# Attention into a gated channel mix: keys and gates from token pairs and projected values

## The chip, the cores and the metric

The kernel runs on one core of one Trainium2 chip. The core has five engines that work side by side, each through its own queue in order: PE (TensorE, matrix products into PSUM), DVE (VectorE) and ACT (ScalarE), which read PSUM and SBUF and write to either, POOL (GpSimd), which here only issues loads, and SP (SyncE), which issues stores. The metric is device time in microseconds, the median of several runs. PSUM has eight banks, each 512 fp32 numbers wide on 128 partitions; whatever PE makes must be read out of a bank before the bank can be used again.

## What is computed

Shapes: 8 batches, 8 heads, 576 tokens, head size 64, 32 memory slots a head. The first half is an attention over memory slots:

```python
a = exp(phi - max(phi)); a = a / a.sum(over slots)     # per token, slot
k_m = einsum('bhsm,bhsd->bhmd', a, k)                  # 32 keys a head
v_m = einsum('bhsm,bhsd->bhmd', a, v)                  # 32 values a head
attn = softmax(q @ k_m.T / 8)                          # 576 x 32 a head
x = (attn @ v_m), heads side by side                   # 576 x 512 a batch
```

The second half is a channel mix, in which every token is mixed with the token before it (zeros before the first):

```python
xk = mu_k * x + (1 - mu_k) * x_prev
xr = mu_r * x + (1 - mu_r) * x_prev
k = relu(xk @ w_k)               # 512 -> 1024, the "keys"
v = (k * k) @ w_v                # 1024 -> 512, the "values"
out = sigmoid(xr @ w_r) * v      # the "gates", 512 -> 512
```

## The kernel before

The order of all work is written out by hand in PLAN, one word a step; a step that has several parts (products, then a read-out, then a second read-out) stands there once for each part. `3:s` is batch 3's score step, `c2:5s` block 5 (of 8) of the keys of chunk 2, `g:7` the gate and `o:7` the value of output tile 7, `p:k:4` the load of k of batch 4, `0:busy7_2` seven filler products. BANKS gives each product's PSUM bank. Steps run on an engine in this order, so a waiting step holds back all behind it on its engine. Loads go through POOL's queue (lines 137, 141, 172, 184), the first of phi and k through ACT's (137, 150), stores through SP's (589), the last ones in turn through SP's and ACT's.

Attention of a batch. The 8 heads are split in two groups c of four; four heads of 32 slots make 128 rows. `exp_phi` (L256, ACT) makes the unnormalised weights `em`. `ekv` (L280) makes slot keys and values, 72 products of 64 x 32 of the array. `esum` (L290) sums the weights, `norm_k`/`norm_v` (L316, L327) scale by the reciprocal. `tr_k` (L346) turns the keys, `turn_q` (L365, DVE) turns q. `scores` (L378) makes 32 products of 32 x 32 of the array and four exponentials of 288 elements (L386, ACT). From batch 1 on the softmax is normalised on DVE: `fold_e` turns the exponentials (L412), `fold_sum` adds and inverts (L418, L419), `fold_out` turns the result back (L424), `weigh` multiplies (L431), twice. Batch 0 takes another way, which is shorter when the engines are idle: `denom` sums on PE (L394), a logarithm and an exponential on ACT (L402, L407) invert.

Channel mix of batches 1 to 7. `values` (L337) makes x = attn @ v_m: eight products of 32 x 64 of the array, twice (the first 320 and the last 256 tokens), and x is copied to SBUF (L445). `diff` (L457, L458, DVE) forms x - x_prev, `mix` scales it by mu - 1 (L468 on ACT or L470 on DVE) and adds x (L472): this gives xkT and xrT, rings of four batches with the 512 features on partitions. Batch 0 skips this: `norm_mu`/`norm_both` (L482, L496) put mu into the slot values, and `mixed` (L337) makes xk and xr directly, which are copied out (L518).

`key` (L604): for 128 of the 1024 key features and up to 512 tokens, four products of 128 x 128 of the array, one for each 128 of the 512 features; then relu (L610 DVE or L612 ACT) and square (L619 ACT or L621 DVE) into `sq`. Chunks after batch 0 are 512 tokens whatever the batch. `gate` (L637): four products of 512 columns for 128 tokens, then tanh (L641, ACT; the sigmoid as a tanh). `value` (L654): eight products of 512 columns for 128 tokens, then one DVE instruction multiplies by the gate (L660), and `store` writes the rows, usually as two pieces of 64.

Of the kernel before, what the change touches and what calls it, by code (L numbers as in the profile page):

```python
# [18 lines left out]
PLAN = [  # L19
    "0:c00d 0:exp1 0:busy1_5 0:exp0 0:q0 0:c01a 0:busy13_9 0:z 0:busy7_2 0:z 0:kg0 p:q:0h 0:mu 0:busy2_3 0:c10d",  # L20
    "0:c11a 0:kg1 0:busy2_1 0:ak 0:busy1_e0 0:tk 0:busy1x7_e2b 0:q1 0:busy1_4 0:busy1x4_4b 0:tk 0:s0 0:s0 0:s1",
    "0:busy1x6_5b p:v:0g 0:s1 0:vg0 0:busy1x5_3b 0:mu 0:l0 0:l0 0:l1 0:mub 0:mub p:v:0h 0:vg1 0:nm1 0:nm0",
    "0:busy1x4_e1b 0:l1 0:r0z 0:w0 0:l2 0:l2 0:busy1x4_2b 0:h2z 0:y2 0:busy1x4_e0b 0:l3 0:l3 0:busy2_e1 0:h3z",
    "0:busy5_0 0:busy2_e0 0:y3 0:mk0 0:uk0d 0:mk1 0:uk0a 0:uk1d p:wk:0-4 c0:0as p:wk:4-8 c0:0as c0:0as 0:mr0 0:ur0a",
    "0:ur0d c0:1av c0:1av c0:1av c0:3av c0:3av c0:3av c0:2a 0:uk1a p:phi:1 1:exp 0:mr1 0:ur1a c0:4bs 0:ur1d c0:6as",
    "c0:6as c0:6bs c0:6bs c0:6bs 1:z 1:z p:k:1 1:k c0:4bs c0:2b c0:2a 1:ak c0:4bs c0:2a c0:3b p:q:1 c0:3b 1:q0 c0:3b",
    "c0:4as 0:busy1x7_e1b c0:4as c0:4as 1:tk 1:tk c0:1bs c0:1bs c0:7as c0:7as 1:q1 c0:5av 1:s c0:7as c0:5av c0:5av",
    "c0:6as 1:s 1:s c0:0bs c0:7b 1:fe 1:fs 1:fo p:wv:0-2 p:wr:0-4 c0:1bs c0:7b c0:7b p:v:1 1:w0 p:wv:2-4 o:0a o:1a",
    "1:w1 0:tb p:phi:2 c0:5b p:k:2 c0:5b c0:2b c0:2b c0:5b g:1 g:1 g:0 g:0 o:0a g:3 g:3 o:1a c0:0bs 1:v 1:av g:2 1:x0",
    "p:v:2 c0:0bs 1:x0 o:3a 1:x0 1:xv1 1:xv1 o:2b o:0b o:3a o:2a o:1b 1:xv1 2:exp 1:dd 1:k0d 1:k0d 2:z 2:z 1:k2e",  # L30
    "1:k2e o:3b g:2 c1:0s c1:0s c1:0s c1:4 c1:4 p:q:2 c1:6 c1:6 c1:5s c1:5s c1:5s c1:3v 2:kv 2:ak o:0b o:3b 2:av o:2b",
    "1:r2d c1:7s c1:7s 2:tk 1:r0d 1:r0d 1:r2d c1:6 c1:7s c1:3v c1:3v 2:q0 2:q1 c1:2 c1:2 g:7 2:tk 2:s c1:4 2:s 2:s",
    "g:7 c1:1s c1:1s c1:1s p:q:3 p:v:3 p:phi:3 g:6 g:8 p:k:3 g:5 g:5 3:exp o:1b c1:2 o:7 o:2a 3:q1 2:fe 2:fs 2:fo",
    "2:w1 2:w0 o:7 o:5 o:5 3:z g:6 g:8 3:z 2:x1 2:x1 2:x1 g:4 2:xv0 p:phi:4 3:kv 3:q0 2:xv0 p:q:4 o:4 3:av 2:xv0 g:4",
    "3:ak 3:tk 2:dd 2:k2e p:phi:5 4:exp 3:tk o:6 2:k0d 2:k0d 3:s 3:s 3:s 2:k2e c2:5s c2:5s c2:4v c2:5s c2:2s c2:6s",
    "c2:6s c2:6s c2:0s c2:0s c2:0s 2:r2d c2:3s c2:3s 2:r0d 2:r0d p:v:4 3:fe c2:3s 2:r2d g:10 3:fs c2:7 c2:2s c2:7 o:6",
    "3:fo o:4 g:11 g:11 3:w1 3:w0 c2:1v g:10 g:9 c2:1v c2:1v c2:7 c2:4v 4:z 4:z 4:q0 c2:4v p:k:4 3:x0 g:12 g:9 3:x0",
    "3:x0 4:kv 3:x1 c2:2s o:11 4:q1 3:x1 3:x1 3:dd 3:k0d 3:k0d o:8 4:av o:11 o:8 o:10 5:exp 4:ak 4:tk 4:tk 5:z 5:z",
    "3:k2e 3:k2e p:v:5 p:k:5 5:kv 4:s g:12 5:ak 5:av c3:0s c3:6s 4:s 4:s 3:r0d 3:r0d o:10 p:q:5 3:r2e 5:q0 5:tk 5:tk",
    "5:q1 c3:4s c3:4s 4:fe 4:fs c3:0s 3:r2e c3:1 5:s 5:s 5:s 5:fe c3:1 p:phi:7 c3:5 c3:0s c3:1 4:fo c3:4s 4:w1 c3:7s",  # L40
    "c3:3s c3:3s c3:3s c3:5 g:14 4:w0 g:14 c3:7s c3:7s c3:2s o:9 o:9 g:16 c3:2s c3:2s c3:6s c3:6s g:13 g:13 4:x0 c3:5",
    "o:14 5:fs 5:fo 5:w0 5:w1 4:x0 4:x0 o:14 g:16 o:15 p:q:6 p:v:6 6:q1 7:exp 4:x1 4:x1 4:x1 4:dd o:13 o:13 4:k0d 7:z",
    "p:v:7 7:z 4:k0d 5:x0 5:x0 5:x0 g:17 p:phi:6 o:12 o:12 4:k2e 4:k2e 5:xv1 g:17 5:xv1 5:xv1 6:q0 5:dd 5:k0d 5:k2d",
    "5:k0d 5:k2d g:15 g:15 6:exp c4:6s c4:6s c4:6s o:15 c4:2s c4:2s c4:2s c4:3s c4:3s p:k:6 c4:0 c4:0 c4:1 c4:1 6:z",
    "6:z 4:r2d 6:kv c4:3s p:k:7 7:kv 7:ak 6:nk 7:av c5:1s c4:5s c4:1 c5:1s c5:1s c4:0 c5:2s 4:r2d c5:2s 6:nv 6:tk",
    "6:tk 5:r0d c4:5s c4:5s c4:4 c4:4 c4:7s c4:7s c4:7s 7:tk 7:tk 6:s 4:r0d c4:4 o:16 4:r0d g:18 p:q:7 7:q1 7:q0 6:s",
    "6:s 6:fe 6:fs 6:fo c5:0s 7:s 5:r2e 5:r2e 5:r0d c5:0s 7:s c5:2s c5:3 c5:6s 6:w1 6:w0 c5:3 o:16 c5:7s c5:0s c5:7s",
    "c5:7s 7:s 7:fe g:20 c5:4v g:19 g:19 c5:3 o:19 o:19 g:20 c5:6s c5:4v c5:4v c5:6s o:17 o:17 6:x1 6:x1 7:fs 7:fo",
    "7:w0 c5:5s c5:5s c5:5s g:18 7:w1 6:x1 o:18 o:18 o:20 o:21 6:xv0 6:xv0 6:xv0 6:dd 6:k0d 6:k0d 6:k2d 6:k2d g:25",
    "g:25 7:x1 7:x1 o:20 7:x1 o:22 7:xv0 7:xv0 g:21 g:21 o:21 7:xv0 7:dd g:23 g:22 c6:0s g:23 c6:7s 6:r0e 6:r0e 6:r2e",  # L50
    "6:r2e c6:1 7:k0d c6:4s c6:4s c6:2v c6:2v 7:k0d 7:k2e c6:3s c6:0s c6:2v g:22 c6:0s 7:k2e o:23 o:22 c6:1 c6:1 g:26",
    "c7:0s c7:0s c6:5s o:23 g:30 c6:6s g:26 c8:1 c7:0s c6:4s c6:7s c6:7s c6:5s c6:5s c7:3 c8:1 g:27 c6:3s c7:1 c6:6s",
    "g:29 c6:3s g:27 g:24 g:24 c6:6s c7:3 c7:5s c7:3 c7:2 c8:6v c7:2 c7:2 7:r2e 7:r2e o:26 o:26 c7:4 c7:4 o:24 c7:5s",
    "o:25 c7:4 c7:5s c8:6v g:28 c8:1 g:30 7:r0e o:24 c8:5 c8:6v 7:r0e g:32 g:35 o:25 c7:1 c8:5 c8:4s c8:4s c8:2 c8:4s",
    "c7:7 c7:1 c8:5 c7:7 g:29 c7:6 c7:6 g:31 g:31 c7:7 c7:6 o:31 o:31 o:29 o:27 c8:7 o:27 g:35 g:34 g:34 c8:2 c8:2",
    "c8:3 c8:3 c8:3 o:29 c8:0 c8:0 c8:0 g:28 o:28 o:28 g:32 o:30 o:30 c8:7 c8:7 o:34 g:33 o:33 o:32 o:34 g:33 o:33",
    "o:32 o:35 o:35 o:35 o:35",
# [3 lines left out]
BANKS = (  # L61
    "0123456701243051623405471624371236745201367452167541260371462317054637105463710472104572630457260340"
    "1401473501473514762305714602357162034576034573425103472503614736145073142507316407216403176240517624"
    "3017620147632014736201475301462537401625301631251760231572460374260374203201574572361527035417521524"
    "7610541534156450643257"
)

PRE = "q:0g id:"
SUMS = ()


NJ = 9
# [5 lines left out]
def kernel(  # L78
# [25 lines left out]
    HALVES = (slice(0, 5 * QR), slice(5 * QR, S))  # L104
    CT = 512
    STARTS = (0,) + tuple(range(S, NTOK, CT))

# [6 lines left out]
    banks = iter(BANKS)  # L114

    def ps_tile(shape, dtype, name):
        bank = next(banks, None)
        return psum.tile(shape, dtype, name=name, tag="ps" + (bank or ""), bufs=1 if bank else 8)
# [28 lines left out]
    k0 = []  # L147
    for gs in (slice(0, 2), slice(2, 4)):
        k0.append(work.tile([128, 2, NJ, D], F32, name="k0f", tag="x", bufs=3))
        nc.scalar.dma_start(out=k0[-1].rearrange("p h j d -> p h (j d)"), in_=rows(k[0])[:, gs])  # L150
# [60 lines left out]
    RING = 4 * S  # L211
    xk_T = big.tile([128, ND, RING], BF16, name="xkT")
    xr_T = big.tile([128, ND, RING], BF16, name="xrT")
    sq = big.tile([128, NF, 2 * S], BF16, name="sq")

    def keep_busy(n, blocks=CT // 64):

        ps = ps_tile([128, CT], F32, "idle")[:, :blocks * 64]
        for _ in range(n):
            nc.tensor.matmul(ps.rearrange("p (a b) -> p a b", b=64), lhsT=zeros,  # L220
                             rhs=zeros[:, :64].unsqueeze(1).to_broadcast([128, blocks, 64]), start=True, stop=True,
                             skip_group_check=True)
# [13 lines left out]
    def load_mu():  # L236
        ps_mu = ps_tile([128, 2 * ND], F32, "psmu")
        nc.tensor.transpose(ps_mu, mu2, ident_f)
        yield
        nc.vector.tensor_scalar_add(mu1, ps_mu, -1.0)  # L240

    def attention(b):
        st = {}

        def half_tile(hf, name):
            sl = HALVES[hf]
            return ps_tile([128, sl.stop - sl.start], F32, name)

        x0 = b * S % RING
# [8 lines left out]
        def cast_k(gs, eng):  # L258

            def go():  # L260
                dst, src = kv5[:, 0, gs], k0[gs.start // 2][:, gs.start % 2:gs.start % 2 + gs.stop - gs.start]
                if eng == "a":
                    nc.scalar.copy(dst, src)
                else:
                    nc.vector.tensor_copy(dst, src)
            return go
# [19 lines left out]
        def esum():  # L286
            st["zps"] = ps_tile([128, 2], F32, "zps")
            parts = [em[:, j].rearrange("p h m -> p (h m)") for j in range(NJ)] if b not in SUMS else st["es"]
# [6 lines left out]

        def sum_rows():

            left = work.tile([128, HH * M], F32, name="es", tag="es", bufs=1)
            nc.vector.reduce_sum(left, em.rearrange("p j h m -> p (h m) j"), axis=mybir.AxisListType.X)
            terms = work.tile([128, 3, HH * M], BF16, name="et", tag="et", bufs=1)  # L300
            for i in range(3):
# [132 lines left out]
        def values(hf, both=False):  # L434

            def go():
# [3 lines left out]
                for i in range(ND):  # L440
                    if i % 2 == 0:
                        yield
# [276 lines left out]
```

## Time and profile before

Three runs took 201.34, 201.42 and 201.59 us, median 201.42. The profile is of one execution, whose span from the first to the last instruction is 199.2 us; what lies around the span is not in it (2.2 us against the median).

| engine | busy us | share of the span | instructions |
|---|---|---|---|
| PE, products | 192.4 | 97% | 2188 |
| PE, weight loads (beside products) | 101.7 | 51% | 2211 |
| DVE | 145.1 | 73% | 302 |
| ACT | 142.6 | 72% | 320 |
| POOL | 28.8 | 14% | 43 |

| group | engine | count | busy us |
|---|---|---|---|
| keys, L604 | PE | 344 | 67.7 |
| values, L654 | PE | 319 | 65.3 |
| gates, L637 | PE | 138 | 35.2 |
| filler, L220 | PE | 122 | 15.5 |
| relu, L612 | ACT | 71 | 38.0 |
| tanh, L641 | ACT | 36 | 21.2 |
| gate times value, L660 | DVE | 41 | 24.8 |

How to read it: busy time is a union, in which overlapping instructions count once; a few records of products are missing (344 of 352 for the keys). The mean time of one instruction is from its start to its own end, and neighbours overlap, so a rate is read from one start to the next. A tile shape such as 64*32 is the part of the array that a product uses. In the table by stretches the columns are the stretch, its length, the busy time (and count) of PE, PEld, DVE, ACT and POOL, PE's granted clock, the DMA share and GB/s; in the timeline, the start, the time covered, engine, line, operation, tiles and count.

### The profile page before, as it was taken

Reading aid. Unit: us, or ns where it says so; the run is one execution under the profiler, and the core shown is the slowest. Engines: PE = TensorE matmul, PEld = TensorE weight load, DVE = VectorE, ACT = ScalarE, POOL = GpSimd, SP = SyncE. Lnnn points to the kernel's source line nnn. Section 1 sums busy time; section 2 is a strip of 40 time slices with the busy share of each in tenths; the row PEclk is TensorE's granted clock in tenths of the full one; section 3 lists DMA queues with packets and bytes.
Section 4 is the critical chain, followed back from the end, with each engine's and each line's share of the span. In section 5 each row is a group of like instructions: output and inputs, shape, how many; then the busy total and the mean of one; then the engine's idle time right before and its main releaser. Section 6 shows DMA issues by size and latency. Waiting matters only on the chain.

```text
span 199.2 us, 5369 instructions
## 1 busy us (share of the span) xinstructions
PE 192.4 (97%) x2188; PEld 101.7 (51%) x2211; DVE 145.1 (73%) x302; ACT 142.6 (72%) x320; POOL 28.8 (14%) x43
## 2 busy tenths in 40 slices
PE   8999999999999999999999999999999999999992
PEld 8445677675444445544446854443444444444451
DVE  2046858898999999999999989997996037232541
ACT  3337899858868899799979999753778978343310
POOL 7553411410117100270000000000000000000000
PEclk9999999999999999999999999999999999999998
DMA  6999999999999999999997010062042202404454
GB/s 205 274 206 263 211 204 203 265 228 225 248 281 293 266 207 252 263 251 255 250 233 188 17 44 0 16 146 53 0 107 56 54 0 65 95 3 105 105 127 137
DMA packets 24521, 31.88 MB, mean 160 GB/s; under 512 B 1960, under 2 KB 19120, under 8 KB 24496
## 3 DMA queue, kind: packets, MB, share of 16 engines
q0 software_dynamic: 16848, 20.32, 53.6%
q1 hardware_dynamic: 6176, 8.92, 17.5%
q10 hardware_dynamic: 1472, 2.29, 3.3%
q8 instruction: 17, 0.28, 0.5%
q14 instruction: 8, 0.07, 0.1%
HBM read 38.28 MB, written 9.44 MB: 240 GB/s over the span
## 4 chain that ended last, share of the span: by engine, by line
PE 84%; DMA 10%; DVE 1%; ACT 1%; issue 1%; POOL 0%
PE pk L604 28%; PE pv L654 26%; PE pr L637 14%; DMA ph<-in_phi_dram 10%; PE idle L220 7%; PE kvps L280 3%; PE nops L337 1%; PE scps L378 1%; DVE xkT L472 1%; PE mxps L337 1%; PE zps L290 1%; ACT em L256 1%; PE ktps L346 1%; ACT sg L641 0%; DVE mu_d L470 0%
## 5 line engine op out<-in xcount | busy, mean ns | idle before, releaser
L604 PE MATMUL pk<-xkT,wk 128*128 128x512 bf16 (+4 forms) x344 | 67.7, 340 | 0.7 <-DVE xkT L472 0.3
L654 PE MATMUL pv<-wv,sq 128*128 128x512 bf16 (+3 forms) x319 | 65.3, 352 | 0.4
L604 PEld LDWEIGHTS <-wk 128*128 128x128 bf16 x352 | 32.8, 98 | 28.1 <-issue 1.8
L654 PEld LDWEIGHTS <-sq 128*128 128x128 bf16 x328 | 31.3, 98 | 29.8 <-issue 0.2
L612 ACT ACTIVATE rl<-pk 128x512 bf16<-128x512 f32 (+3 forms) x71 | 38.0, 555 | 10.8 <-PE pk L604 10.4
L637 PE MATMUL pr<-wr,xrT 128*128 128x512 bf16 x138 | 35.2, 379 | 0.5 <-ACT sg L641 0.2
L660 DVE SCALAR_TENSOR_TENSOR o<-sg,pv 128x512 f32<-128x512 f32 (+3 forms) x41 | 24.8, 616 | 10.8 <-PE pv L654 10.2
L641 ACT ACTIVATE sg<-pr 128x512 f32<-128x512 f32 x36 | 21.2, 597 | 14.0 <-PE pr L637 9.9
L621 DVE TENSOR_TENSOR sq<-rl 128x512 bf16<-128x512 bf16 (+5 forms) x45 | 14.6, 344 | 18.5 <-ACT rl L612 17.6
L619 ACT ACTIVATE sq<-rl 128x512 bf16<-128x512 bf16 (+5 forms) x59 | 26.8, 488 | 0.9
L637 PEld LDWEIGHTS <-xrT 128*128 128x128 bf16 x144 | 13.6, 98 | 16.1 <-DVE xrT L472 0.2
L445 ACT CAST x<-nops 128x256 bf16<-128x256 f32 (+1 forms) x46 | 15.2, 413 | 7.1 <-PE nops L337 7.1
L468 ACT ACTIVATE mu_d<-diff,mu 128x576 bf16<-128x576 bf16 x22 | 15.8, 782 | 1.7 <-DVE diff L458 1.4
L220 PE MATMUL idle<-zeros 128*128 128x64 bf16 (+4 forms) x122 | 15.5, 293 | 1.0 <-DVE zeros L151 1.0
L365 DVE STREAM_TRANSPOSE qT<-q 128x576 uint32<-128x576 uint32 x16 | 12.1, 764 | 4.2 <-DMA q<-in_q_dram 4.2
L386 ACT ACTIVATE e<-scps 128x288 bf16<-128x288 f32 x32 | 10.6, 413 | 1.9 <-PE scps L378 1.9
L431 DVE TENSOR_TENSOR atn<-e,lz 128x576 bf16<-128x576 bf16 (+2 forms) x17 | 11.4, 716 | 0.1
L470 DVE TENSOR_SCALAR mu_d<-diff,mu 128x576 bf16<-128x576 bf16 x34 | 11.3, 382 | 0.1
L256 ACT ACTIVATE em<-ph 128x1152 bf16<-128x1152 f32 (+1 forms) x9 | 9.5, 1070 | 2.6 <-DMA ph<-in_phi_dram 2.6
L457 DVE TENSOR_TENSOR diff<-x 128x1024 bf16<-128x1024 bf16 (+1 forms) x21 | 10.4, 552 | 0.7 <-ACT x L445 0.2
L472 DVE TENSOR_TENSOR xrT<-x,mu_d 128x1152 bf16<-128x1152 bf16 x14 | 10.2, 745 | 1.0 <-ACT mu_d L468 0.9
L220 PEld LDWEIGHTS <-zeros 128*128 128x128 bf16 x122 | 8.3, 120 | 5.0 <-issue 1.1
(68 smaller groups left out, 149.1 us busy)
## 6 DMA issues: line engine op xcount, KB each, us to landing
out_dram<-o SPq DMA_DIRECT2D x59, 128.0 KB, 2.4
ph<-in_phi_dram POOLq DMA_DIRECT2D x7, 576.0 KB, 18.8
kv<-in_k_dram POOLq DMA_DIRECT2D x7, 576.0 KB, 17.7
q<-in_q_dram POOLq DMA_DIRECT2D x7, 576.0 KB, 19.9
kv<-in_v_dram POOLq DMA_DIRECT2D x7, 576.0 KB, 16.2
k0f<-in_k_dram ACTq DMA_DIRECT2D x2, 576.0 KB, 7.0
wk<-in_moe_w_k_dram POOLq DMA_DIRECT2D x2, 512.0 KB, 13.3
wv<-in_moe_w_v_dram POOLq DMA_DIRECT2D x2, 512.0 KB, 18.8
```

The source lines that it names most:

```text
L220: nc.tensor.matmul(ps.rearrange("p (a b) -> p a b", b=64), lhsT=zeros, rhs=zeros[:, :64].unsqueeze(1).to_broadcast([128, blocks, 64]), sta ...
L445: (nc.vector.tensor_copy if both and i > 1 else nc.scalar.copy)(st["x"][:, i, sl], pss[i])
L468: nc.scalar.activation(t[:, i], st["d"][:, pr + i, :], AF.Copy, scale=mu1[:, o:o + 1])
L472: nc.vector.tensor_add(dst, st["x"][:, pr:pr + n], t)
L604: nc.tensor.matmul(pk[:, p0 - lo:p1 - lo], lhsT=wk_sb[:, di, fi * 128:(fi + 1) * 128], rhs=xk_T[:, di, p0 % RING:p0 % RING + p1 - p0], sta ...
L612: nc.scalar.activation(rl, pk, AF.Relu, scale=HALF ** 0.5)
L619: nc.scalar.activation(sq[:, fi, p:p + p1 - p0], rl[:, part], AF.Square)
L621: nc.vector.tensor_mul(sq[:, fi, p:p + p1 - p0], rl[:, part], rl[:, part])
L637: nc.tensor.matmul(pr, lhsT=xr_T[:, di, c0:c0 + 128], rhs=wr_sb[:, di, :], start=(di == 0), stop=(di == ND - 1))
L641: nc.scalar.activation(gated[t], pr, AF.Tanh, scale=0.5)
L654: nc.tensor.matmul(pv[:, cols], lhsT=sq[:, fi, p:p + 128], rhs=wv_sb[:, fi, cols], start=(fi == 0), stop=(fi == NF - 1))
L660: nc.vector.scalar_tensor_tensor(o[:, cols], in0=gated[t][:, cols], scalar=1.0, in1=pv[:, cols], op0=AL.add, op1=AL.mult)
```

## The change

The keys and gates of batches 1 to 7 are no longer computed from x. With A the softmax weights of a token (256 numbers, 8 heads x 32 slots) and V the slot values, x = A V, so xk @ w_k = A G0 + A_prev G1, where G0 = V (mu w_k), Gs = V w_k and G1 = Gs - G0. Tokens are taken in pairs (a, b), where p is the token before a: b's result is A_a Gs + (A_b - A_a) G0, and a's is A_a Gs + (A_p - A_a) G1. The product A_a Gs is shared, so a pair takes three products over 256 slots instead of two over 512 features.

- `tr_v` turns the slot values, `project` multiplies them with w_k, w_r (Gs) and with mu w_k, mu w_r (G0), six steps a batch, each eight products of 64 x 32 of the array and 512 columns into two banks; `keep_g` copies each bank into `G` on ACT or DVE; `other_g` subtracts G1 on DVE (three a batch). `scale_w` makes mu w_k and mu w_r once, on DVE.
- The tokens of batches 1 to 7 stand in two halves of 288, all a's and all b's: `exp_scores` writes the exponentials in that order, 16 instructions of 64 or 80 elements a batch in place of 4 of 288. `steps_between` forms the two differences of weights (DVE, four instructions).
- `pair_key`: two products of 288 columns make the shared part in one bank; ACT or DVE copies it to a second bank; two products more go onto each bank. `relu` then reads each bank by itself, `square` takes both at once. `pair_gate` is the same for 128 pairs and 512 columns. The last 32 tokens of each half do not fill a tile: `rest_gate`, and `value` for tiles named e0 to e3, take those of two batches together, four pieces of 32 columns of the array each.
- Removed for these batches: `values` into x, `diff`, `mix`, the rings xkT and xrT. Kept for batch 0: `mixed`, keys and gates from x0T.
- Batch 0's scores, exponentials, logarithms and products go by token halves and not by head groups (`s0`, `s1`, `es00` ...). Filler products after the warm-up run: 16 in place of 44.
- An output tile of batches 1 to 7 is stored as four pieces of 32 rows. The last steps (TAIL) use SP's and ACT's queue in turn.
- All steps have a new place, bank and engine in PLAN (`c2:1/a@4`: on ACT, bank 4); the loads have a new order, and wk comes in three pieces.

The diff, cut to its core:

```diff
-    "1:w1 0:tb p:phi:2 c0:5b p:k:2 c0:5b c0:2b c0:2b c0:5b g:1 g:1 g:0 g:0 o:0a g:3 g:3 o:1a c0:0bs 1:v 1:av g:2 1:x0",
...
+    "2:s@5602 2:G00@41 2:es1 g:11 2:E000/d 2:es0 t:111 g:10@0 2:Gs0@24 s:16/d 2:G02@56 t:110 2:fe p:k:4 o:11@7 2:fs",
+    "2:fo g:10/a@3 g:10 2:Es01/a o:13@4 2:w0 2:E021/a o:12@6 2:E020/a o:13 t:101 2:w1 o:11 t:100 2:Es00/a c2:1@0",
+    "c2:2@2 2:Gs2@34 2:E001/a 2:D0 2:Gs1@15 o:e0@7 4:exp 2:Es21/d 2:Es11/a 2:Es10/a c2:1/a@4 2:Es20/a 2:G01@15 o:12",
...
+            if b:
+                e = st["e"][:, c].rearrange("p (r v u) -> p r v u", r=2, u=PB)
+                for w in range(2):
+                    ps = st["sc", 0][c, w].rearrange("p j (u r) -> p r j u", r=2)
+                    for r, vs, js_ in EVEN_ODD:
+                        nc.scalar.activation(e[:, r, vs, w * PB // 2:(w + 1) * PB // 2], ps[:, js_[0], js_[1]],
+                                             AF.Exp, scale=scale)
...
+        def project(v, i):
+            def go():
+                pss = [ps_tile([128, CT], F32, "gps", cover=CT) for _ in range(2)]
+                w = ((wk_sb, wr_sb), (mwk, mwr))[v == 0][i == 2]
+                cols = GCOLS[i % 2] if i < 2 else slice(0, Dm)
+                for g in range(HH):
+                    m = slice(g * M, (g + 1) * M)
+                    for c in range(2):
+                        nc.tensor.matmul(pss[c][m], lhsT=st["vT"][ROWS[c], m], rhs=w[ROWS[c], g, cols],
+                                         start=True, stop=True, skip_group_check=True)
...
+        def keep_g(v, i, c):
+            return lambda: copier()(g_tile()[:, v, c, GCOLS[i]], st["gps", v, i][c])
+        def other_g(i):
+            return lambda: nc.vector.tensor_sub(g_tile()[:, 1, :, GCOLS[i]], g_tile()[:, 2, :, GCOLS[i]],
+                                                g_tile()[:, 0, :, GCOLS[i]])
+        def steps_between():
+            d = st["d"] = work.tile([128, 2, 2, NP], BF16, name="diff", tag="diff", bufs=2)
+            a = st["at"].rearrange("p c (r i) -> p c r i", r=2)
+            nc.vector.tensor_sub(d[:, 1], a[:, :, 1], a[:, :, 0])
+            nc.vector.tensor_sub(d[:, 0, :, PB:], a[:, :, 1, :NP - PB], a[:, :, 0, PB:])
...
-                        nc.tensor.matmul(pk[:, p0 - lo:p1 - lo], lhsT=wk_sb[:, di, fi * 128:(fi + 1) * 128],
-                                         rhs=xk_T[:, di, p0 % RING:p0 % RING + p1 - p0],
-                                         start=(di == 0), stop=(di == ND - 1))
...
+    def pair_key(b, fi):
+        def go():
+            f = slice(fi * 128, (fi + 1) * 128)
+            pa = ps_tile([128, NP], F32, "pk", cover=NP)
+            for c in range(2):
+                nc.tensor.matmul(pa, lhsT=st["G"][:, 2, c, f], rhs=st["at"][:, c, :NP], start=c == 0, stop=False,
+                                 skip_group_check=True)
+            yield
+            pb = ps_tile([128, NP], F32, "pb", onto=NP)
+            copier()(pb, pa)
+            yield
+            for ps, (v, kind) in zip((pa, pb), SHIFTS):
+                for c in range(2):
+                    nc.tensor.matmul(ps, lhsT=st["G"][:, v, c, f], rhs=st["d"][:, kind, c], start=False, stop=c == 1,
+                                     skip_group_check=True)
...
+    def rest_gate(n):
...
+            for k in range(4):
+                for w in range(4):
+                    nc.tensor.matmul(ps[w * PB:(w + 1) * PB], lhsT=terms[w][k][0], rhs=terms[w][k][1], start=k == 0,
+                                     stop=k == 3, skip_group_check=True)
...
+            b, (h, r) = int(name[0]), divmod(int(name[1]), 2)
+            for v in range(4):
+                parts.append((out[b].rearrange("(u x) d -> x u d", u=PB)[8 * h + 2 * v + r], v * PB, PB))
+        for n, (dst, p, rows_) in enumerate(parts):
+            queues[n % len(queues)].dma_start(out=dst[:, cols], in_=o[p:p + rows_, cols])
```

## The prediction

> **What bounds the kernel now.** I read the page's busy shares and slices first, then the busy time by stretches, then the timeline. The page:
> ```profile
> span 199.2 us, 5369 instructions
> ...
> PE 192.4 (97%) x2188; PEld 101.7 (51%) x2211; DVE 145.1 (73%) x302; ACT 142.6 (72%) x320; POOL 28.8 (14%) x43
> ...
> PE   8999999999999999999999999999999999999992
> ```
> PE is full in every slice, so two things count: the work that PE must do, and what makes it wait. The stretches (busy time of PE, PEld, DVE, ACT, POOL) show PE full even where the others nearly are:
> ```profile
> 20.00:60.00 40.00, 39.28 (x587) 24.37 (x587) 33.96 (x71) 32.99 (x78) 8.58 (x12) 1.00 1.23 234
> 60.00:100.00 40.00, 39.58 (x520) 18.88 (x525) 38.96 (x74) 36.48 (x88) 9.45 (x13) 1.00 1.17 254
> ```
> From 60 to 100 us DVE is busy 38.96 of 40 us and ACT 36.48, and PE still 39.58. The timeline gives prices; I take them from one start to the next, since neighbours overlap:
> ```profile
> 94.77 1.89 PE L637 MATMUL pr<-wr,xrT 128*128 128x512 bf16 x8
> 96.58 0.34 PE L337 MATMUL nops<-atn,vb 32*64 32x320 bf16 x8
> 96.86 3.63 PE L654 MATMUL pv<-wv,sq 128*128 128x512 bf16 x15
> ...
> 47.80 0.80 PE L280 MATMUL kvps<-kv,em 64*32 64x128 bf16 x72
> ...
> 84.84 0.52 ACT L327 ACTIVATE vb<-kvps,rz 128x64 bf16<-128x64 f32 x2
> 85.24 1.33 ACT L386 ACTIVATE e<-scps 128x288 bf16<-128x288 f32 x4
> 86.40 1.49 ACT L468 ACTIVATE mu_d<-diff,mu 128x576 bf16<-128x576 bf16 x2
> ...
> 95.91 1.35 DVE L418 TENSOR_REDUCE se<-eT 128x36 f32<-128x1152 bf16 x1
> 97.29 0.38 DVE L419 RECIPROCAL se<-se 128x36 f32<-128x36 f32 x1
> 97.70 1.38 DVE L424 STREAM_TRANSPOSE lz<-se 128x1152 f32<-128x1152 f32 x1
> ```
> A 512-column product costs 0.216 us (8 `pr` with 0.09 behind them in 1.81), so 0.422 ns a column. Eight tiled `nops` of 320 columns take 0.28, not 8 x 0.135: they run side by side. 72 `kvps` of 128 columns take 0.73, where nine rounds of eight side by side are 0.49: eight 64x32 tiles run together too. A tiled run costs a fixed 0.23 (0.09 ahead of it, 0.14 after). ACT: four `e` of 288 elements from PSUM in 1.16, so 0.29; 512 take 0.48; hence 0.05 + 0.84 ns an element. DVE: 512 from PSUM 0.60, the 1024 bf16 `diff` 0.60, a 576 bf16 product 0.36.
>
> **The change part by part.** PE, over all batches:
> - keys: 147456 columns (62.2 us) become 18432 for batch 0 (7.8) and 7 batches x 8 blocks x 6 products x 288 columns (40.8): -13.6.
> - gates: 144 x 0.216 = 31.1 become 16 for batch 0 (3.5), 84 in pairs (18.1) and four leftover gates of four side-by-side rounds (3.5): -6.0.
> - values: the same columns; the leftover tiles run as four 32-wide pieces side by side: 0.
> - projections G: 42 of eight 64x32 tiles at 512 columns, 42 x 0.216 = +9.1; transposes of v +0.8.
> - `values` into x gone: -1.7. Tiled runs, counted in the order of the two plans, 36 become 49: 13 x 0.23 = +3.0.
> These terms give before 178.4 (its products fill 179.7 in the trace: 1.3 us of waits, kept) and after 170.0: **-8.4**. One filler product at 27.3 us goes: -0.2.
>
> Start: scores, exponentials and logarithms of batch 0 go by halves of its tokens.
> ```profile
> 13.77 0.50 PE L378 MATMUL scps<-qT,kmT 32*32 32x288 bf16 x32
> ...
> 19.01 1.02 PE L337 MATMUL mxps<-atn,vmm 32*64 32x320 bf16 x40
> ...
> 20.08 0.80 PE L604 MATMUL pk<-xkT,wk 128*128 128x320 bf16 x4
> ```
> With scores at 13.8, ACT runs exp 4 x 0.18, ln 0.32, exp 2 x 0.16, exp 0.38, ln 0.32, exp 2 x 0.16, exp 0.38, and DVE's product (0.49) ends near 17.5; today the mixing starts at 19.0. The second half's logarithms and the four copies of the first keys' input, now all on ACT (1.06), give most of it back: first key at 19.5, not 20.1: -0.6 (0 to -1.5).
>
> End: a 128-token tile leaves as four stores of 32 rows, not two of 64; SP takes 0.47 to 0.6 us for each today. 18 a batch are 10 us beside 21 of PE, hidden. But after the last batch's second value tile SP still has 18 to issue, 9.9 us at 0.55, and PE 7.6 us of work; the last store starts 2 us after PE's end, today 0.4: +1.5 (0.5 to 2).
>
> Without new waits: 201.4 - 8.4 - 0.2 - 0.6 + 1.5 = **193.7**. The sum is made on the span of 199.2; the 2.2 us from it to the median of 201.42 stay as they are.
>
> ACT and DVE lie beside PE and cost nothing while they keep up. ACT: x copies -13, scaling -15, relus -9, squares -12, 75 G copies x 0.48 = +36, copies to the second bank 43 x 0.29 + 12 x 0.48 = +18, exponentials +4: 131 to 138. DVE: shift differences -11, scaling -9.5, sums -19, 21 G differences x 0.60 = +12.6, token steps +7, relus +15, squares +5, the rest +12: 142 to 154. Per batch that is ACT 17.5, DVE 19.7, PE 20.9. The row from 60 to 100 us hides such shares, but there is no slack to recover with. PE takes its work in order, so all behind a waiting product stands. Three new waits:
>
> (a) The softmax chain. A batch's first pair product needs its weights: exponentials on ACT, then on DVE transpose, sum, reciprocal, transpose and two products (5.3 us by the rows, up to 7.1 with what the plan queues among them). The 16 exponentials per batch, of 64 or 80 strided PSUM elements, have no row. The line above gives 0.10 to 0.115; `vb`, nearest in size, 0.20; a `vb` that overlaps nothing 0.33. `vb` carries a per-partition scale; `mu_d` with one (0.67 for 576) against a square without (0.58) puts that at 0.09, so I take 0.11. Chain against the PE work that the plan puts over it, batches 1 to 7: 9.4/10.6, 8.2/8.4, 9.8/9.9, 10.1/11.3, 8.4/10.0, 10.0/9.4, 8.1/9.2: +0.6. At 0.20 each chain is 1.4 longer and the sum of the excesses 5.2; at 0.24 it is 9.9.
> The Trainium skill (ScalarE: Activation LUTs, What ACT_TABLE_LOAD costs) gives an ACTIVATE 186 ns + 0.833 ns an element, with about 93 ns overlapped: 0.15 to 0.16 here. For 288 elements it says 0.33, where the trace has 0.29. By it the chain costs 2.4 and the total comes out 1.8 higher, at 198.5.
>
> (b) The copy between a pair's products. PE's second group needs it: drain 0.16, start 0.03, copy 0.41, hand-over 0.05, together 0.65. Of 70 such copies 26 have under 1.0 us of PE work over them. If the copying engine is free each time this costs 0.4; if it must first do everything that the plan puts between, 14.7. I take 1.3, near the lower end: the row from 60 to 100 us shows PE hardly waiting for engines that full.
>
> (c) PSUM banks. 84 G copies (0.48 or 0.60) empty what PE fills two at a time in 0.22 to 0.45; the plan puts value products between. 0 to 3, I take 1.1.
>
> Loads: POOL's queue waits eight loads deep and lands one each 2.7 us. By its new order `wr` lands at 29.3 (needed at 30.4), v of batch 1 at 32.2 (33.0), `wv` at 34.8 (36.1). Cover 0.8 to 1.3; what lands later than that costs as much.
>
> The sum: 193.7 + 0.6 + 1.3 + 1.1 = **196.7**; its own range 194.5 to 199.5.
>
> **The rivals.**
> 1. Slower: the chain alone. Exponentials that do not overlap, 0.24: 193.7 + 2.4 + 9.9 = 206.0. The place is PE's wait before each batch's first key; it decides from 0.20 each (5.3 us of waits). For it: `vb`'s 0.20 and the strided source; against: the line through 256, 288, 320 and 512.
> 2. DVE becomes the bound. At whole durations (512 from PSUM 0.68, 288 relu 0.45) a batch needs 21.6 of it, 0.7 over PE, with 0.1 for hand-overs: 7 x 0.8 more, 202.3. Against: 38.96 of 40, hidden.
> 3. Tiles do not run together at 512 columns. G at half rate: +9.1, 205.8. Against: `kvps`; no row has 128x32 tiles.
> 4. PE's clock falls at the start. Filler products after the warm-up go from 44 to 16, and PE idles some 2.4 us ahead of the second half of k, which lands at 10.7. In this trace 512-column fillers ran 0.42 us apart until 6.4 us and 0.216 after; a second slow spell of 3 to 6 us around the first keys costs 2 to 3: 199.3. Against: 2.4 us of idling is less than the warm-up took.
> The Trainium skill (TensorE: Matmul & The Clock Gate, Part 1) halves the clock after an idle window of about 3.4 us; the gap stays under that, and no trace here has such a gap.
> 5. The gain is eaten by (b) and (c), 7.7 in all: 201.4.
>
> **How the numbers follow.** Likeliest 0.48; rivals 0.10, 0.19, 0.05, 0.10 and 0.08. A change of 0.2% (0.4 us) is about what a measurement of this kernel can tell from none. Faster: the likeliest, 4 and a little of 5, 0.61; same 0.05, from 5; slower 0.34: 1, 2, 3. The range of 194 to 205 takes in all but rivals 1 and 3 and a run with no new wait.
>
> **What would show it.** Product time by line: keys 49 us, pair and leftover gates 25, G 9 plus 0.23 a run; first key at 19.5; the small exponentials 0.11 from start to start; PE idle 4 to 5 us after the first key, most of it before a batch's first key or inside a pair. The prediction is wrong if the exponentials take 0.15 or more, if G's projections stand over 0.5 apart back to back, if DVE is over 96% busy through the middle with PE waiting for it, or if the clock is below full after 10 us.

## The result

The changed kernel takes 203.43 us (median of 4, 202.97 to 203.62), the kernel before 201.50 in the same job: ratio 1.0093, 95% interval 1.0079 to 1.0108. It is 0.9% slower. Here and below a median takes in every run of a kernel, and a ratio only those within 1.5% of its fastest run. The forecast was 196.7 us; the time lies in the range of 194 to 205, on the side that had 0.34. The profile below is of the 202.97 run, whose mean granted clock is 0.976; the other three have 0.959.

### The profile page after: what moved, and what is told of

Its sections match the earlier page's. It is cut to its first block, busy times and chain, and to the rows that moved or that the text cites. A ratio compares the mean times of both kernels' runs of the same rounds, so it can differ in the third digit from the quotient of the medians.

```text
span 201.0 us, 6598 instructions
## 1 busy us (share of the span) xinstructions
PE 187.4 (93%) x2650; PEld 106.4 (53%) x2650; DVE 158.8 (79%) x352; ACT 152.3 (76%) x434; POOL 29.3 (15%) x44
## 4 chain that ended last, share of the span: by engine, by line
PE 72%; ACT 10%; DVE 10%; DMA 3%; issue 2%; ACTq 1%; DVEq 0%
PE pv L749 26%; PE pk L619 6%; PE pk L627 6%; PE pb L627 5%; PE gps L493 4%; PE pk L601 4%; PE kvps L318 3%; ACT e L420 3%; DMA k0f<-in_k_dram 3%; PE pr L679 3%; PE pr L671 2%; PE pb L679 2%; PE pv L743 2%; DVE rl L587 2%; ACT rl L585 2%; PE idle L251 2%
## 5 line engine op out<-in xcount | busy, mean ns | idle before, releaser
L749 PE MATMUL pv<-wv,sq 128*128 128x512 bf16 (+1 forms) x288 | 60.3, 356 | 0.3 <-DVE sq L593 0.2
L499 ACT CAST G<-gps 128x512 bf16<-128x512 f32 x75 | 40.5, 640 | 5.2 <-PE gps L493 4.9
L627 PEld LDWEIGHTS <-G 128*128 128x128 bf16 x224 | 21.3, 97 | 8.0 <-issue 1.0
L627 PE MATMUL pk<-diff,G 128*128 128x288 bf16 x112 | 22.9, 286 | 0.0
L627 PE MATMUL pb<-diff,G 128*128 128x288 bf16 x112 | 22.9, 286 | 0.0
L593 DVE TENSOR_TENSOR sq<-rl 128x576 bf16<-128x576 bf16 (+2 forms) x49 | 20.6, 438 | 1.8 <-ACT rl L585 0.7
L623 ACT COPY pb<-pk 128x288 f32<-128x288 f32 x43 | 16.6, 398 | 5.7 <-PE pk L619 4.0
L619 PE MATMUL pk<-atn,G 128*128 128x288 bf16 x112 | 20.3, 286 | 0.0
L585 ACT ACTIVATE rl<-pk 128x288 bf16<-128x288 f32 (+2 forms) x39 | 16.2, 419 | 3.8 <-PE pk L627 2.0
L420 ACT ACTIVATE e<-scps 128x80 bf16<-128x80 f32 (+1 forms) x112 | 15.0, 320 | 0.1
L619 PEld LDWEIGHTS <-G 128*128 128x128 bf16 x112 | 10.6, 98 | 5.5
L601 PE MATMUL pk<-x0T,wk 128*128 128x256 bf16 (+1 forms) x64 | 10.9, 326 | 0.0
```

The costliest lines, as they stand in the source:

```text
L420: nc.scalar.activation(e[:, r, vs, w * PB // 2:(w + 1) * PB // 2], ps[:, js_[0], js_[1]], AF.Exp, scale=scale)
L499: return lambda: copier()(g_tile()[:, v, c, GCOLS[i]], st["gps", v, i][c])
L585: nc.scalar.activation(rl, ps, AF.Relu, scale=HALF ** 0.5)
L593: nc.vector.tensor_mul(dst, rl, rl)
L601: nc.tensor.matmul(pk, lhsT=wk_sb[:, di, fi * 128:(fi + 1) * 128], rhs=xk_T[:, di, sl], start=(di == 0), stop=(di == ND - 1))
L619: nc.tensor.matmul(pa, lhsT=st["G"][:, 2, c, f], rhs=st["at"][:, c, :NP], start=c == 0, stop=False, skip_group_check=True)
```

## The profile after

The page of the kernel after (span, busy times, slices of PE and of the granted clock):

```profile
span 201.0 us, 6598 instructions
...
PE 187.4 (93%) x2650; PEld 106.4 (53%) x2650; DVE 158.8 (79%) x352; ACT 152.3 (76%) x434; POOL 29.3 (15%) x44
...
PE   8498798989999999999999999999999999999990
...
PEclk9999579999999999999999999999999999999997
```

PE is busy 5.0 us less than before (192.4), and yet the span is 1.8 longer. The loss is in the first nine slices: PE was full there before and is not now, and the clock falls to half in the fifth and for a part of the sixth. The same by stretches (busy time of PE, PEld, DVE, ACT, POOL, then clock, DMA share and GB/s):

```profile
20.00:60.00 40.00, 37.55 (x663) 24.65 (x663) 32.76 (x86) 32.01 (x90) 8.64 (x12) 0.91 1.16 221
60.00:100.00 40.00, 39.82 (x501) 20.73 (x494) 37.63 (x75) 35.30 (x102) 5.33 (x8) 1.00 1.00 218
100.00:140.00 40.00, 39.79 (x483) 21.78 (x482) 36.24 (x74) 35.31 (x104) 3.71 (x5) 1.00 0.68 142
```

From 60 us on PE is full, with DVE at 37.6 of 40 us: what was feared of the new steady state (chain, copies, banks, DVE) does not show. The timeline of the start (start, duration, line, what waited):

```profile
10.27 3.63 PE L251 MATMUL idle<-zeros 128*128 128x512 bf16 x9
...
13.82 0.45 PE L318 MATMUL kvps<-kv,em 64*32 64x64 bf16 x36
...
20.96 0.43 PE L361 MATMUL mxps<-atn,vm 32*64 32x256 bf16 x4 [0.48 <-DVE atn L466]
21.96 0.75 PE L361 MATMUL mxps<-atn,vm 32*64 32x256 bf16 x20 [0.57 <-issue]
...
22.64 1.67 PE L601 MATMUL pk<-x0T,wk 128*128 128x256 bf16 x7
```

The first key stands at 22.64 us; before it was 20.08, and the forecast 19.5. Three things are to be seen. The nine fillers ahead of the second half of k take 3.55 us to the next start (in e1 below, at full clock, 1.94), since the clock is at half until 13.68 us (0.42 us each), so this half, cast by 10.9 us, waits for them until 13.8. In the middle of the mixing PE stands still for "issue", that is for nothing that the trace shows. And the seven keys take 1.67 us, 0.24 each instead of 0.11: the clock is at half again, from 20.51 to 27.34.

## Experiments

**1 to 4: the clock.** Fillers behind the warm-up (e1), in the mixing (e2), both (e3), and the gap made in the kernel before (e4). The fillers of e2 and e3 share a bank with one of batch 0's mixing sums, and their output is not the kernel's, so these two are read for their time alone.

```diff
 e1, e3, PLAN:
-0:exp1 0:z@0 0:z
+0:exp1 b:10x8 0:z@0 0:z
 e2, e3, PLAN (and in mixed(0, 0): keep_busy(1 + s) behind each part; in mixed(0, 1): four of 192 columns):
-0:l01@0
+b:2x8@6 0:l01@0
 e4, PLAN of the kernel before:
-0:busy13_9
+0:busy1_9
```

> The kernel after, with ten filler products of 512 columns put between the warm-up and the first sums, where PE lay idle from 5.1 to 8.2 us. Theory A (clock: the gap keeps the granted clock at half until 13.7 us, and the nine fillers ahead of the second half of k, 0.42 us each, hold back the keys' chain): full clock from about 6.9 us, the second half of k's products at 11.5 to 12 us instead of 13.8, the first key at about 20.5 instead of 22.6, 200 to 201.5 us in all; the second half-clock spell (20.5 to 27.3 us) may stay. Theory B (the new kernel's waits for copies, banks and the softmax chain took the gain, and the start is late because of its loads and casts): within 0.4 us of 203.4.

> The kernel after, with filler products only where PE waits between 18.6 and 22 us (two of 512 columns ahead of the last sums, three in and behind the first mixing, four of 192 in the second). Theory A: the start stays as it is (full clock from 13.7 us, first key at about 22.6), but the half-clock spell from 20.5 to 27.3 us is gone, and the 4.7 us of keys and mixing that lay in it take half: 201 us. Theory B: within 0.4 us of 203.4.

> Both sets of fillers. Theory A: full clock from about 6.9 us on without a break, first key at about 20.3 us, 198 to 199.5 us. Theory B: within 0.4 us of 203.4.

> The kernel before with the 13 fillers of 512 columns behind its warm-up cut to one, so that PE is idle from about 5.6 to 8.6 us as in the kernel after. Theory A: the clock is full only from about 13.7 us instead of 6.6, and the time rises by 2 to 3 us to about 204. Theory B: within 0.5 us of 201.5, since the start waits for its loads either way.

Measured: e1 201.22 us (200.39 to 202.25; ratio to before 0.9984, 0.9962 to 1.0006), e2 202.01 (1.0042, 1.0014 to 1.0070), e3 201.92 (200.04 to 204.55; ratio 0.9984, 0.9956 to 1.0012), e4 201.62 (1.000, 0.999 to 1.001). So e1 gives 2.2 of theory A's 2 to 3.4 us, e2 1.4 of 2.4, and theory B is out; but the two do not add up. e4 did not make the gap that it was meant to make:

```profile
6.53 0.39 PE L290 MATMUL zps<-ones,em 128*128 128x2 bf16 x9 [0.34 <-ACT em L256]
...
10.79 0.44 PE L280 MATMUL kvps<-kv,em 64*32 64x64 bf16 x36 [1.26 <-DVE kv L265]
```

With its 12 fillers gone the first sums start at 6.53 instead of 8.86, and PE's idle time falls into pieces of 1.26 us at most, where the kernel after has one of 2.86. Its time says that the kernel before can do without these fillers; what a gap of 2.9 us would cost that kernel was not measured. The start of e1:

```profile
9.41 1.96 PE L251 MATMUL idle<-zeros 128*128 128x512 bf16 x9
...
11.35 0.44 PE L318 MATMUL kvps<-kv,em 64*32 64x64 bf16 x36
...
19.61 0.51 PE L361 MATMUL mxps<-atn,vm 32*64 32x63 bf16 x30 [1.28 <-issue]
```

The second half of k comes 2.5 us earlier, as theory A has it, but the pause in the mixing has grown to 1.28 us, and the clock falls at 20.42 for one window. Its windows (same columns as above):

```profile
13.60:17.01 3.41, 2.82 (x142) 1.82 (x143) 0.63 (x3) 2.79 (x12) 2.07 (x3) 1.00 1.30 203
17.01:20.42 3.41, 1.53 (x49) 0.74 (x49) 2.33 (x8) 2.16 (x9) 1.08 (x2) 1.00 1.23 291
20.42:23.83 3.41, 2.97 (x35) 1.77 (x35) 1.09 (x4) 1.79 (x7) 1.51 (x2) 0.50 1.21 214
```

In every trace the clock changes only at steps of 3.413 us, and these start anywhere: the first full clock comes at 3.68 (e2), 5.55 (e3), 6.77 (e1) and 13.68 us (after). Against these windows I set the use of the array: the columns of all products that start in the window, each times its share of the 128 x 128 cells, times 0.422 ns, over 3.413 us. Ahead of a trace's first record of the clock it is half: the fillers stand 0.42 us apart there.

| window | clock, then next | PE busy | use of the array |
|---|---|---|---|
| after 6.86 to 10.27 | half, half | 0.61 | 0.11 |
| after 10.27 to 13.68 | half, full | 1.00 | 0.46 |
| after 13.68 to 17.10 | full, full | 0.95 | 0.49 |
| after 17.10 to 20.51 | full, half | 0.74 | 0.23 |
| after 20.51 to 23.92 | half, half | 0.70 | 0.30 |
| e1 13.60 to 17.01 | full, full | 0.83 | 0.30 |
| e1 17.01 to 20.42 | full, half | 0.45 | 0.17 |
| e6 8.08 to 11.49 | half, half | 1.00 | 0.29 |
| e4 3.25 to 6.67 | half, full | 0.90 | 0.40 |
| e4 10.08 to 13.49 | full, full | 0.68 | 0.48 |

Busy time does not sort them (0.68 stays full, 0.74 falls, and 1.00 does not raise it), the array's use does: over all 14 traces a window of 0.38 or more raised the clock and none of 0.37 or less did; 0.27 or less halved it and 0.36 or more kept it. Of the six windows between, those of 0.30 and 0.318 kept it and those of 0.309, 0.310, 0.316 and 0.320 halved it. Products of 32 x 32 or 32 x 64 cells keep PE busy and count for next to nothing. In e4 each window of the start has 0.40 or more from 3.25 us on. This is a sorting of what was seen; no run changed the use alone. The Trainium skill (TensorE: Matmul & The Clock Gate, Part 1) says that the window of about 3.4 us is free-running and that a kernel's warm-up therefore varies from run to run: the traces agree. Its condition for halving, an idle window, is not what they show: a window in which PE was busy for 74% was enough.

**5: the pause.** Fewer, wider products in the warm-up, so that 136 instructions less stand ahead of the mixing.

```diff
-WARM = (78, 1)
+WARM = (10, 8)      # with e1's fillers
```

> The kernel after with the ten fillers of the run that filled the gap behind the warm-up, and its warm-up as 10 filler products of 512 columns instead of 78 of 64: nearly the same columns, 136 instructions fewer on PE ahead of the mixing. In the kernel after PE stands still for 0.7 us inside batch 0's mixing, with the filled gap for 1.3 us, for nothing that the trace shows as a wait: 10 products earlier in the filled kernel, which has 10 products more ahead of it, so both times after the same number of PE instructions. Theory F (PE waits for its own instructions there): the pause moves 68 products on, into the keys, the first key comes at 19.6 to 20.0 us instead of 20.9, and the time is 0.5 to 1.5 us below the 201.2 of the filled kernel. Rival (a wait between two particular products): the pause stays between the same two products of the mixing, 201.2 within 0.4.

Measured 203.16 us, 1.9 slower than e1. PE in e5:

```profile
14.56 0.41 PE L404 MATMUL scps<-qT,kmT 32*32 32x128 bf16 x30
16.73 0.23 PE L404 MATMUL scps<-qT,kmT 32*32 32x128 bf16 x2 [1.75 <-issue]
```

The pause left the mixing, which speaks against the rival; but it went into the scores, not on into the keys. Counting PE's rows in the traces (products, weight loads, and its semaphore and drain instructions) settles it. The pause stands behind row 705 in the kernel after and in e1, behind row 449 in e5, and e5 has a second one behind row 2497, within one batch's slot keys:

```profile
78.98 1.41 PE L318 MATMUL kvps<-kv,em 64*32 64x128 bf16 x138
82.34 0.24 PE L318 MATMUL kvps<-kv,em 64*32 64x128 bf16 x6 [1.95 <-issue]
```

705, 449 and 2497 are all 449 and a multiple of 256. The DMA records hold packets of 16384 bytes of kind "instruction" (64 bytes for each of 256), one for each such block: it started at 19.59 us in the kernel after and PE went on at 21.96, in e1 17.34 and 19.61, in e5 14.53 and 16.73, then 79.86 and 82.34: 2.2 to 2.5 us each time. PE waits for its own program where it comes to the end of a block less than that after the next block's packet has started; at the later block ends of the kernel after it comes 3.4 us or more after it and does not stand. How long the block lasts does not decide it alone: e5's 256 rows up to 2497 passed in 1.2 us, but the block up to row 705 lasted 4.9 us in the kernel after, and a later one of 4.15, whose packet had started at once, cost nothing. The price in e5 is its two pauses of about 2 us against e1's one of 1.3. What sets the start of a fetch stays open: in e5 it came between 1.6 us before and 4.6 us after PE entered the block ahead.

**6: the end.** The stores of the last batch's tiles on two queues.

```diff
-t:700 o:70 o:73@3 t:711 o:73 t:701
+t:700 t:711 t:701 o:70 o:73@3 o:73
-TAIL = ("o:71", "o:e3a", "o:e3b",)
+TAIL = ("o:70", "o:73", "o:71", "o:e3a", "o:e3b")
```

> The kernel after, with the stores of the last batch's first and last full tiles put on SP's and ACT's queues in turn (today only the last tile and the leftover tile), and the three gates ahead of them in ACT's order. In the kernel after SP's last store starts 2.6 us after DVE's last product, in the kernel before 0.4 us after it. Tail theory (the prediction's +1.5 for stores of 32 rows): 1.3 to 1.7 us less, 201.7 to 202.1. Rival (the landing of the last store sets the end, whoever issues it): within 0.3 of 203.4.

Measured 201.51 us (200.68 to 201.79; ratio to before 0.9992, 0.9978 to 1.0007): 1.9 us less. The end of the kernel after, queue of SP and DVE's last product:

```profile
192.75 6.03 SPq L732 DMA_DIRECT2D out_dram<-o  x10
...
195.84 0.35 DVE L755 SCALAR_TENSOR_TENSOR o<-sg,pv 128x192 f32<-128x192 f32 x1 [0.42 <-PE pv L743]
```

SP still issues at 198.8, 2.6 us after DVE ended at 196.2; in e6 DVE ends at 195.46 and the last store starts at 196.08. From PE's end to the span's it is 3.95 us before, 5.19 after and 3.92 in e6. The rest of the gain is PE's own earlier end (195.05 for 195.79 us in the two profiles), with the half-clock windows at other places.

**7: all of it, on e5's short stream.**

```diff
 e5 and e6, and in PLAN:
-0:s1@0123 0:l10@6
+0:s1@0123 b:1x6 0:l10@6
-0:l11@7
+0:l11@3
-0:l01@0
+b:2x8 0:l01@6
-0:mk0@2130
+0:mk0@2103
-0:mk1@4576
+b:2x8 0:mk1@4576
```

> Filled gap, short warm-up stream, the shared tail, and filler products at three places of batch 0's chain where PE waits anyway (six blocks ahead of the second half's first sums, two products of 512 columns ahead of the last sums, two between the first two mixings). If clock, instructions and tail are the causes they add up: 203.4 - 2.2 - 1 - 1.5 = 198.7, less up to 1 us if the half-clock spell at 20 us goes too: 197.5 to 199.2. If the new kernel's copies, banks and chain hold the time, it stays above 200.5.

Measured 201.50 us (199.71 to 204.57), a miss: the expectation still took a short stream for a gain. It has e5's two pauses, of 1.9 and 1.7 us, behind the same rows 449 and 2497.

**8: the softmax chain.**

```diff
-    nc.scalar.activation(e[...], ps[...], AF.Exp, scale=scale)
+    for _ in range(2):
+        nc.scalar.activation(e[...], ps[...], AF.Exp, scale=scale)
```

> The kernel after with each of the 112 small softmax exponentials of batches 1 to 7 issued twice (16 more of 0.11 us on ACT in each batch's chain). The prediction's model of the chain (0.6 us of excess at 0.11 each, 5.2 at 0.20, 9.9 at 0.24) gives 7 us more, about 210.5. Rival (the chain has slack that the model did not see, since PE runs ahead elsewhere): under 2 us more, 205.4 or less.

Measured 243.25 us. The test hit harder than meant: the second exponential writes what the first wrote and waits for its end, so a pair takes 0.385 us from start to start, not 0.22, and each chain is 16 x 0.275 = 4.4 us longer. PE stands and waits for it, here ahead of a gate of batch 0:

```profile
36.72 1.02 PE L659 MATMUL pr<-wr,x0T 128*128 128x512 bf16 x4 [0.27 <-ACT e L421]
41.33 1.02 PE L659 MATMUL pr<-wr,x0T 128*128 128x512 bf16 x4 [3.58 <-ACT e L421]
```

After the first key 21.5 us of PE's idle time end with these exponentials, about 3.1 of the 4.4 us a chain; the mean clock, 0.892 instead of 0.976, is there for the rest of the 40 us. So the rival of a hidden slack is out. The slack comes to about 1.3 us a chain (an estimate: 4.4 less 3.1), where the prediction's chains and covers gave 0.7 on average.

**9 to 12: what they are worth together.** e9 is e1 and e6 and nothing else; e10 adds e7's fillers and banks; e11 lengthens e10's stream ahead of the mixing by 28 rows, e12 shortens e9's by 40.

```diff
 e11:
-WARM = (78, 1) ... b:10x8
+WARM = (94, 1) ... b:8x8
 e12:
-WARM = (78, 1) ... b:10x8
+WARM = (56, 1) ... b:12x8
```

> The kernel after with the filled gap behind the warm-up and the shared tail, and nothing else: instruction blocks of 256 end where they did in the run with the filled gap alone (at PE rows 449 and 705), so one pause of 1.3 us in the mixing stays. If the two gains add up: 203.4 - 2.2 - 1.9 = 199.3, below the kernel before by 1%. If they overlap (the same time counted twice) it stays at 201.

> The same with filler products at three places of batch 0's chain (six blocks, two products of 512 columns, two of 512), which are to keep the array's use per 3.4 us above the 0.39 under which no window so far raised the clock, and the banks of three steps exchanged so that the fillers' bank is free. Theory A (clock): the half-clock spell at 17 to 20 us, seen in the profile of the filled kernel, goes in most executions: 198.3 to 199.3. Rival (fillers in a chain of waits only delay it): 199.3 or more.

> The same again, with 16 more narrow filler products in the warm-up and two wide ones fewer behind it: 28 more rows of PE's stream ahead, so that PE's row 705 is the first product of the mixing (where PE waits for ACT anyway) and not one in its middle. Theory F (a block of 256 instructions is waited for where it ends): the pause of about 1.3 us inside the first mixing becomes one of about 0.7 at its start, 0.5 us below the dense kernel. Rival (a pause of its own there): no difference from the dense kernel.

> The kernel with the filled gap and the shared tail, with 22 narrow filler products fewer in the warm-up and two wide ones more behind it: 40 rows of PE's stream fewer ahead of the mixing, so that PE's row 705 falls in the last third of the second mixing and no longer in the middle of the first. Theory F (PE waits at rows 449 + 256 k for its next block of instructions): the step of over 1 us is at row 705 again, but behind the first mixing, whose copies on ACT and DVE then run during the pause; the first key comes 0.3 to 0.7 us earlier than in the run with filled gap and tail alone, and the time is 198.9 to 199.4 against 199.6. Rival (a pause that belongs to the first mixing): it stays at the same product, 199.6.

Measured: e9 199.60 us (198.68 to 201.01), ratio to before 0.9909 (0.9875 to 0.9942): with 1.9% less than the kernel after it beats both. e10 200.95 (0.9946, 0.9919 to 0.9973), e11 202.45 (1.0037), e12 200.36 (0.9931, 0.9906 to 0.9955). So the gains of e1 and e6 add up (199.3 was expected). e10's profiled execution has no half-clock window between 5.17 us and the end of PE's work, and a span of 196.6:

```profile
PEclk9999999999999999999999999999999999999999
```

but its other executions take up to 203.48 us: the fillers can keep the clock up, as theory A has it, and do not do so reliably. The expected 198.3 to 199.3 was missed. The mean clock on record for the others is 0.974 to 0.994 against 0.999, so they did have half-clock windows, but it does not order them: 203.48 us has 0.981 and 202.40 has 0.974. What else they lose its one trace does not show. In e11 and e12 the pause stood behind row 705 again, as theory F says, at the start of the first mixing and in the middle of the second one:

```profile
19.48 0.80 PE L361 MATMUL mxps<-atn,vm 32*64 32x256 bf16 x14 [0.36 <-DVE atn L466]
21.14 0.52 PE L361 MATMUL mxps<-atn,vm 32*64 32x64 bf16 x10 [0.85 <-issue]
```

(this is e12). It is behind row 705 in ten of the fourteen traces, whatever product stands there: in all of the kernel after and its variants but e5 and e7 with their shorter stream. Its size was not as expected: 1.8 us in e11 for the 0.7 I gave, with a second one of 1.1 at 83.77 us, and in e12 the block end at row 449 took 1.0 of its own. So neither shift gained: e11 is 1.5 us slower than e10, and e12 missed its 198.9 to 199.4. The place of a pause could be foretold, its price not.

## Why the prediction was wrong

The forecast's span, 194.5 us, in three parts, beside the kernel after:

| | forecast | after |
|---|---|---|
| first key at | 19.5 | 22.64 |
| first key to PE's end | 169.55 | 173.15 |
| PE's end to the span's end | 5.45 | 5.19 |

- **The step that failed is the start, "-0.6 (0 to -1.5)"**, and with it rival 4 in the words "2.4 us of idling is less than the warm-up took". The first key came 2.6 us later than before, not 0.6 earlier. Of the 3.1 us against the forecast, about 2.5 are the fillers at half clock (second half of k at 13.82, in e1 at 11.35); the pause for instructions takes 0.6 in the kernel after and 1.3 in e1, where it eats a part of what e1 won. The rest of the forecast chain fits: e1's first key at 20.86 less its pause would stand at 19.6, an estimate that no run shows. Whether leaving the nine fillers out would do as well as keeping the clock up for them was not run.
- **The clock after that**: from the first key to PE's end it is 171.3 us in e10 and 171.0 in e2, both at full clock, so about 1.8 of the 173.15 are the half-clock spell. "Below full after 10 us" was one of the prediction's own signs of being wrong. Rival 4 had the mechanism at 2 to 3 us and a chance of 0.10; it cost about 2.5 ahead of the keys and 1.8 in them. What I compared was the length of one gap; what sorts the traces is the array's use in windows that lie anywhere, and batch 0's small tiles have next to none.
- **PE's work, -8.4**: mis-sized. Products from the first key on fell by about 5.7 (175.15 to 171.3, and 1.8 more that new waits fill). Pair keys take 42.9 us for 40.8: nine products ahead of a run of small tiles take 0.215 and not 0.1215, and some wait. The 42 G projections take 14.4 to the next start, 0.34 each, where I had 0.216 and a fixed cost for 13 more runs in all. Tiles of 128 x 32 do run four at a time (a leftover gate's four rounds stand 0.22 apart, first line below), so rival 3 is out.

```profile
192.53 1.05 PE L701 MATMUL pr<-G,atn 128*32 128x512 bf16 x16
...
193.40 1.26 PE L743 MATMUL pv<-wv,sq 128*32 128x320 bf16 x32
...
59.98 2.08 ACT L420 ACTIVATE e<-scps 128x80 bf16<-128x80 f32 x16
61.76 0.79 ACT L648 ACTIVATE sg<-pb 128x512 f32<-128x512 f32 x1
```

- **Waits, +3.0**: about 1.8 (PE's idle time after the first key that another engine ends, 2.5 against 0.7 before), most of it before 45 us. (a) The small exponentials take 0.118 and 0.104 us from start to start for 80 and 64 elements (16 in 1.78 us, last two lines above); I had 0.11, so rival 1 is out. The Trainium skill (ScalarE: Activation LUTs, What ACT_TABLE_LOAD costs) made them 0.15 to 0.16; the trace has less. Rival 2: DVE is at 37.63 of 40, and PE full. Rival 5 is out: (b) and (c) are within these 1.8.
- **The end, +1.5**: 1.24, shown by e6.
- **ACT and DVE**: from the page's 142.6 and 145.1 the terms of the prediction add up to 151.6 and 157.2, not to its 131 to 138 and 142 to 154. The kernel after has 152.3 and 158.8. What PE waited for them is within the 1.8.

That the time lies in the range is luck: the clock, the one rival that came, was put at 199.3, and the pause for instructions was in no term.

With the gap filled and the stores shared the change is a gain, though less than half of the forecast one: e9 stands 1.9 us below the kernel before, with one pause and some half-clock windows left.

## What to carry to other kernels

A start that waits for loads is not free to fill or to leave empty: what its small tiles do to the clock and to the instruction stream is paid by the dense work behind it, and shows only when the clock's windows are laid over the array's use and not over PE's busy time. A pause that the trace puts to nothing is worth counting in instructions: if it stays at the same count while the work ahead of it changes, it is the program's own fetch. Where a change cuts stores into smaller ones, count what is left to issue when the last product ends, and share it between queues.

## What the runs showed of the hardware

- The granted clock changes at steps of 3.413 us whose start differs from run to run, and the use of the array's cells in such a window sorts the changes: 0.38 and more raised it, 0.27 and less halved it. The times of one kernel with a sparse start lie up to 5.1 us apart (e10: 198.41 to 203.48), those of the kernel before up to 1.0; that the place of the windows makes this difference fits, but was not shown.
- PE's instructions come in blocks of 256, and where PE had to wait for one it went on 2.2 to 2.7 us after the block's packet had started: coming to a block's end sooner, among small-tile products above all (256 rows in as little as 1.2 us), it stood for 0.6 to 2 us, at rows 449 + 256 k.
- Two activations that write the same elements do not overlap: 0.385 us for a pair whose single ones take 0.11 from start to start.
